# Two layers of local attention and a token-mixing MLP on one core: the last output projection summed in two parts, residual rows loaded in place, probability rows padded in DRAM

## The chip, the cores and the metric

One core of a Trainium2 chip runs the whole program. The metric is device time in microseconds of one launch. Several runs of a kernel are compared by their medians; a profile is one further execution, recorded by the hardware.

## The reference

Four residual blocks on a sequence of 2048 rows of 1024 numbers (bf16): attention A, MLP B, A, B, each after a layer norm.

```python
x = x + _A_ref(_layernorm(x), A_wqkv, A_wo)
x = x + _B_ref(_layernorm(x), B_w1, B_b1, B_w2, B_b2)
x = x + _A_ref(_layernorm(x), A_wqkv, A_wo)
x = x + _B_ref(_layernorm(x), B_w1, B_b1, B_w2, B_b2)
```

`_A_ref` has 32 heads of 32 numbers. A position s looks at the 8 positions s, s-2, ..., s-14: 8 logits, a softmax, a weighted sum of 8 values, then the product with `wo`. `_B_ref` mixes along the sequence: `u = gelu(h^T w1 + b1)` with 3584 hidden numbers for each of the 1024 columns, `y = u w2 + b2`, transposed back.

## The kernel before

Because the attention's step is 2, even and odd positions never meet: the kernel holds them as two classes (`c` = 0 and 1) of 1024 rows, eight row tiles of 128 each. Rows of a layer-normed class are turned into `hT` (features on partitions).

**Attention.** The 1024 features are eight feature tiles (`dt`), in two groups of four; a class and a group make a step n = 0 to 3 of `Attn.stream`. For a step, TensorE (PE) projects q, k and v per feature tile (`project`, L398 to L416; ScalarE, ACT, copies each bank out). `qk` (L431): VectorE (DVE) multiplies q by four windows of k into a tile T, twice per feature tile, and PE sums T over the head's 32 features by a 0/1 matrix `sel` into the logits `sc` (L444). `softmax_front` and `softmax_back` (L449, L458) turn these into probabilities Pb on DVE and ACT. Pb goes to a DRAM scratch `pd` and is read back twice by POOL's queue as `pb` (`spread`, L474), spread over the partitions of each head: 16 rows of 16 KB in `pd`, each read by eight partitions. `pv` (L485) multiplies `pb` by windows of v on DVE and adds up eight products (L500 to L506) into `oT`, the attention output with features on partitions, in two halves (`hf`) of 512 positions. The work of `pv` for step n-1 lies beside `qk` of step n; the PV of the last step stands alone at the end of the stream.

**Output projection.** `out_proj` (L591) computes, for each of eight row tiles, two sums (one for each 512 columns) of eight matmuls over the eight `oT` tiles, into a PSUM bank each; DVE adds the residual row `xr` (L626 or L629), POOL's queue stores the row to `xa`, and the row is normalized into `h2`, by ACT (class 0, `on_act`) or by DVE (class 1). There are six banks in the pool `ps`, shared by all such sums. Class 0's projection lies beside attention of class 1; class 1's follows the last PV.

**MLP.** `gemm1` sums over row tiles of `h2`; the sums over class 0's rows for ten of fourteen blocks are done early (`partials`), as filler. `gemm2_tile` (L670) makes a row tile of the output from 28 hidden tiles in two banks, and adds bias and residual `xs` into `xo` on DVE (L687). In layer 0 class 0's tiles come first and class 1's are filler beside layer 1's attention.

**What sets the order.** `weave` (L715) goes through the attention's units in a plan with guessed costs: units `"pe"` and `"dve"` carry a cost, names they wait for, names they set. Where a unit must wait in the plan, it pulls filler (class 1's rows and values, class 0's output projection, the partial sums) until PE's planned time has come. The plan only ranks the work: a scheduler then orders each engine's instructions, and each engine runs its own in that order. DMAs are issued in order by queue: SP issues all loads and transposes, POOL the stores, `pd` and `pb`. An issue that has to wait for a buffer holds up what is queued behind it.

**Buffers.** Five weight buffers (`wb`: class 1's value weights `wv`, `wo`, `w1`, `w2`), three of `wq`, four row buffers (`x2`: `xr`, `xn`, `xs`, `xo`, `hb`), two for T and the PV products, two of `pb`. Each pool goes round in turn.

Of the kernel before, what the change touches and what calls it, by code (L numbers as in the profile page):

```python
# [26 lines left out]
def kernel(  # L27
# [37 lines left out]
    HF = FT // NW2  # L65
    SLACK = 0.5
    PB_LAG = 12.0
    OUT0_GAP = 7.0
    assert D == H * DH and W == 8 and SC == 1024 and HD * KD == H and SB * CH == 32
    scale = float(DH) ** -0.5  # L70
# [98 lines left out]

    xa = [[dram.tile([SC, D], BF16, name=f"xa{li}{c}") for c in range(DIL)] for li in range(2)]  # L170
    xb = [dram.tile([SC, D], BF16, name=f"xb{c}") for c in range(DIL)]
    pd = [dram.tile([P, W * TB], BF16, name=f"pd{n}") for n in range(2 * DIL * NCQ)]

    xin_v = x_in.rearrange("(i m c) d -> c i m d", m=P, c=DIL)
    out_v = out2d.rearrange("(i m c) d -> c i m d", m=P, c=DIL)
# [173 lines left out]
    class Attn:  # L349
# [81 lines left out]
        def qk(self, n, dq):  # L431
            c, dt = n // NCQ, (n % NCQ) * DQ + dq
            if dq == 0:
                self.sc = pssp.tile([P, 2, 4, TB], FP32, name="sc", tag="sc")
            q, k = self.q_of(c, dt), self.k_of(c, dt)
            for par in range(2):
                yield "dve", 2.2, [("ready", 0, dt), ("ready", 1, dt)], [("free", x, dt % 2) for x in range(2)] if par and not self.apart(c, dt) else [], 0.0, 0.6
                T = tpl.tile([P, 4, SC], BF16, name="T", tag="T")
                nc.vector.tensor_tensor(out=T[:], in0=q.unsqueeze(1).to_broadcast([P, 4, SC]),  # L439
                                        in1=window(k, par, 2, [(2, 4), (1, SC)]), op=ALU.mult)  # L440
                for sb in range(SB):
                    for gr in range(4):
                        b = SB * gr + sb
                        nc.tensor.matmul(self.sc[32 * gr:32 * gr + 32, par], lhsT=sel[:, sb * DQ + dq, :],  # L444
                                         rhs=T[:, :, b * TB:(b + 1) * TB],
                                         start=(dq == 0 and sb == 0), stop=(dq == DQ - 1 and sb == SB - 1))
# [11 lines left out]
        def softmax_back(self, n):  # L458
            yield "dve", 3.0, ["exp"], [("pb", n, 0)], PB_LAG, 0.0
            yield "dve", 0.0, [], [("pb", n, 1)], PB_LAG + 6.0, 0.0  # L460
            nc.vector.tensor_tensor(out=m4[:], in0=L[:, 0:4, :], in1=L[:, 4:8, :], op=ALU.add)
            nc.vector.tensor_tensor(out=m4[:, 0:2, :], in0=m4[:, 0:2, :], in1=m4[:, 2:4, :], op=ALU.add)
            nc.vector.tensor_tensor(out=m4[:, 0, :], in0=m4[:, 0, :], in1=m4[:, 1, :], op=ALU.add)
            nc.vector.reciprocal(out=m4[:, 1, :], in_=m4[:, 0, :])
            nc.vector.tensor_tensor(out=Pb[:], in0=L[:], in1=m4[:, 1:2, :].to_broadcast([P, W, TB]), op=ALU.mult)
            base = self.pd(n)[0, 0]
            dst = bass.AP(base.tensor, base.offset, [(W * TB, 4 * SB), (4 * SB * W * TB, CH), (1, W * TB)])
            nc.gpsimd.dma_start(out=dst, in_=Pb[:].rearrange("p u t -> p (u t)"))
            self.spread(n)

# [3 lines left out]
        def spread(self, n):  # L474


            for hf in range(2):
                pb = pbp.tile([P, 4, W, TB], BF16, name="pb", tag="pb")
                self.pbs[(n, hf)] = pb
                base = self.pd(n)[4 * hf, 0]  # L480
                src = bass.AP(base.tensor, base.offset, [(4 * SB * W * TB, CH), (0, P // CH), (1, 4 * W * TB)])
                nc.gpsimd.dma_start(out=pb[:].rearrange("p b u t -> p (b u t)"), in_=src)

        def pv(self, n, half, hf, dqs=(0, 1)):
# [3 lines left out]
            for dq in (2 * half + x for x in dqs):  # L488
# [20 lines left out]
        def stream(self, lead):  # L509
# [77 lines left out]
            for half in range(2):  # L587
                for hf in range(2):
                    yield from self.pv(last, half, hf)

    def out_proj(at_, c, res, dst, h2, on_act):  # L591

        if not on_act:
            yield "pe", 0.0, ["oT"], [], 0.0
        dst_v = rows(dst)
        wo_t = [[None, None] for _ in range(NDC)]
        for n in range(NDC):
            for hf in range(2):
                wt = wb("wo", [P, KD // 2, 512])
                nc.sync.dma_start(out=wt[:], in_=wo_v[hf, :, :, n * 512:(n + 1) * 512])  # L600
                wo_t[n][hf] = wt
        for hf in range(2):
            h2[c][hf] = hx(f"h2{c}{hf}", [P, NT // 2, D])
        xrs = []

        def fetch():
            if len(xrs) < NT:
                xrs.append(x2("xr"))
                nc.sync.dma_start(out=xrs[-1][:], in_=res[len(xrs) - 1])

        fetch()
        fetch()
        for i in range(NT):
            if not on_act:
                yield "pe", 3.5, ["oT"], [], 3.6
            xr = xrs[i]
            xn = x2("xn")
            s1 = st("s1", [P, NDC]) if on_act else None
            for n in range(NDC):
                ps = bank()  # L620
                xs_ = slice(n * 512, (n + 1) * 512)
                for kt in range(KD):
                    nc.tensor.matmul(ps[:], lhsT=at_.oT[c][kt][:, i * P:(i + 1) * P], rhs=wo_t[n][kt // 4][:, kt % 4, :],  # L623
                                     start=(kt == 0), stop=(kt == KD - 1))
                if on_act:
                    nc.vector.scalar_tensor_tensor(out=xn[:, xs_], in0=ps[:], scalar=1.0, in1=xr[:, xs_], op0=ALU.mult,  # L626
                                                   op1=ALU.add, accum_out=s1[:, n:n + 1])
                else:
                    nc.vector.tensor_tensor(out=xn[:, xs_], in0=ps[:], in1=xr[:, xs_], op=ALU.add)  # L629
            fetch()  # L630
            nc.gpsimd.dma_start(out=dst_v[i], in_=xn[:])  # L631
            h = h2[c][i // 4][:, i % 4, :]
            if on_act:
                nm, rs = stats_act(xn[:], 1.0 + EPS, eps2, h, s1)
                norm_act(h, xn[:], nm, rs)
                yield 3.5, 0.0
            else:
                mean, rs = stats_dve(xn[:], 1.0 + EPS, eps2)
                norm_dve(h, xn[:], mean, rs)

    def w1_tile(c, fb):
        t = wb("w1", [P, NT, FB])
# [25 lines left out]
                    nc.scalar.activation(out=gs, in_=tmp[:], func=ACT.Gelu_apprx_tanh, bias=b1_sb[:, ft:ft + 1])  # L668
                yield 0.216 * nk, 0.0

    def gemm2_tile(c, i, w2t, src, dst, hT, on_act=False, end=False):
        xs = x2("xs")
        nc.sync.dma_start(out=xs[:], in_=src[c][i * P:(i + 1) * P, :])
        xo = x2("xo")
        halves = [slice(n * 512, (n + 1) * 512) for n in range(NDC)]
        groups = [halves[:1], [slice(512, 768)], [slice(768, 1024)]] if end else [halves]
        for cols in groups:
# [7 lines left out]
                    yield 1.5 * len(cols), 0.0  # L685
            for ps, xc in zip(acc, cols):
                nc.vector.scalar_tensor_tensor(out=xo[:, xc], in0=ps[:, 0:xc.stop - xc.start], scalar=b2_sb[:, i, c:c + 1],  # L687
                                               in1=xs[:, xc], op0=ALU.add, op1=ALU.add)
# [25 lines left out]
    def run(*its):  # L714
        for _ in chain(*its):  # L715
            pass

    def weave(lead, fills, lags):
# [6 lines left out]
        def pull(force=False):  # L725
# [13 lines left out]
                        opened[y] = when[f]  # L739
            return False  # L740

        def reach(t):
            nonlocal pe
            while pe < t - SLACK:
                if not pull():
                    pe = min([t] + [x for x in list(opened.values())[:1] if x > pe])
            pe = max(pe, t)

        for kind, *unit in lead:
# [7 lines left out]
                pe, dve = unit  # L757
            elif kind == "pe":
                cost, waits, sets, then = unit
                reach(max([pe] + [when.get(w, 0.0) for w in waits]))  # L760
                pe += cost
                when.update((x, pe + 2.0) for x in sets)
                if then:
                    dve = max(dve, pe) + then
            else:
                cost, waits, sets, lag, then = unit
                dve = max([dve] + [when.get(w, 0.0) for w in waits]) + cost
                if then:
                    reach(dve)
                    pe += then  # L770
# [11 lines left out]
    for li in range(2):  # L782
# [21 lines left out]

        def second_class():
            new_hT(hT, 1)
            for i in range(NT):
                if first:
                    prologue_tile(1, i, hT)
                    yield 0.0, 2.0 * (i % 2 == 0)  # L810
                else:
                    yield from gemm2_tile(1, i, w2_tiles(i), xa[0], xb[1][i * P:(i + 1) * P, :], hT, on_act=i < NT - 2)

        def v_ahead():
            if not first:
# [18 lines left out]
        if first:  # L834
            with at(top):
                ln_exp_table()
            hT = [[None, None] for _ in range(DIL)]
            new_hT(hT, 0)
            for i in range(NT):
                run(gemm2_tile(0, i, w2_tiles(i), xa[0], xb[0][i * P:(i + 1) * P, :], hT))  # L840
        else:
            for i in range(NT):
                w2t = w2_tiles(i)
                for c in range(DIL):
                    run(gemm2_tile(c, i, w2t, xa[1], out_v[c, i], None, end=(i == NT - 1 and c == DIL - 1)))


# [28 lines left out]
```

## Time and profile before

| | |
|---|---|
| median of 17 runs | 1321.79 us (1317.19 to 1325.72) |
| profiled execution | 1317.19 us, its span 1315.4 us |
| mean granted TensorE clock | 0.992 of full |
| PE, DVE, ACT busy | 1279.4, 682.5, 439.3 us |
| moved by DMA | 173 MB |

A page gives busy times, a chain of work, groups of instructions and DMA issues. The timeline gives each stretch of like instructions with its start and length in us, and in brackets how long the engine had stood before it and what released it. The list of waits adds these up: total, times, longest. Engines work beside one another, so an idle engine costs time only where its work sets the end.

### The profile page before, as it was taken

The numbers are of one execution on the slowest core, as the hardware profiler recorded it, in microseconds if no ns is written. First come the engines' busy times: TensorE is split into PE (matmuls) and PEld (weight loads), VectorE is DVE, ScalarE is ACT, GpSimd is POOL, SyncE is SP. The second block draws the span as 40 slices with busy tenths as digits, with TensorE's granted clock in tenths as the row PEclk, the third lists the DMA queues.
The fourth block names the chain that finished last, engine by engine and source line by source line (L and its number), as shares of the span: only waits on it lengthen the run. The fifth ranks groups of instructions, "written<-read, shape, count | busy, mean of one in ns | idle before, by whom it ended". The sixth has DMA issues, their size and how long they took to land. (4 is left out here: it accounts for less than half of the span.)

```text
span 1315.4 us, 15470 instructions
## 1 busy us (share of the span) xinstructions
PE 1279.4 (97%) x6284; PEld 575.7 (44%) x6284; DVE 682.5 (52%) x861; ACT 439.3 (33%) x740; POOL 61.2 (5%) x166
## 2 busy tenths in 40 slices
PE   9998899998999999999999999999899999999999
PEld 5343343443444444444444444444344444444444
DVE  6879789989202332334697844879940033111011
ACT  6844355731313420023534435475132144000000
POOL 3000001000000000000000000010000000000000
PEclk9998899999999999999999999999999999999999
DMA  9752426552523238863659862348262322334332
GB/s 256 168 124 62 112 81 168 176 152 96 145 66 95 76 112 219 218 173 119 165 148 237 213 177 64 88 129 216 73 184 65 85 76 72 118 100 135 118 110 69
DMA packets 243544, 173.00 MB, mean 132 GB/s; under 512 B 32208, under 2 KB 227152, under 8 KB 241424
## 3 DMA queue, kind: packets, MB, share of 16 engines
q1 hardware_dynamic: 233648, 133.45, 37.5%
q0 software_dynamic: 9248, 37.51, 10.2%
q8 instruction: 49, 0.80, 0.3%
q10 hardware_dynamic: 576, 1.05, 0.2%
q14 instruction: 23, 0.19, 0.1%
HBM read 146.81 MB, written 18.87 MB: 126 GB/s over the span
## 5 line engine op out<-in xcount | busy, mean ns | idle before, releaser
L682 PE MATMUL ps<-g,w 128*128 128x512 bf16 (+1 forms) x1820 | 389.7, 376 | 2.8 <-DVE xo L687 2.8
L656 PE MATMUL ps<-h,w 128*128 128x512 bf16 x1792 | 388.1, 379 | 2.7 <-ACT h L230 2.4
L682 PEld LDWEIGHTS <-w 128*128 128x128 bf16 x1820 | 177.5, 98 | 213.1 <-issue 6.1
L656 PEld LDWEIGHTS <-w 128*128 128x128 bf16 x1792 | 175.3, 98 | 214.9 <-issue 3.9
L409 PE MATMUL ps<-hT,wq 128*128 128x512 bf16 (+1 forms) x1112 | 243.8, 376 | 1.0 <-issue 0.5
L667 DVE TENSOR_TENSOR tmp<-ps,g 128x512 f32<-128x512 f32 x80 | 55.3, 692 | 233.1 <-PE ps L656 233.1
L687 DVE SCALAR_TENSOR_TENSOR xo<-ps,b_sb,xs 128x512 bf16<-128x512 f32 (+1 forms) x65 | 45.6, 738 | 247.7 <-PE ps L682 237.0
L439 DVE TENSOR_TENSOR T<-q,k 128x4096 bf16<-128x4096 bf16 x60 | 135.9, 2287 | 67.0 <-ACT q L413 54.0
L409 PEld LDWEIGHTS <-wq 128*128 128x128 bf16 x1112 | 108.8, 100 | 131.4 <-issue 13.8
L504 DVE TENSOR_TENSOR pr<-pr 128x2048 bf16<-128x2048 bf16 (+1 forms) x128 | 119.2, 947 | 0.1
L409 PE MATMUL ps<-hT,wv 128*128 128x512 bf16 x448 | 104.0, 385 | 5.7 <-DMA wv<-in_A_wqkv_dram 5.7
L623 PE MATMUL ps<-wo,oT 128*128 128x512 bf16 x384 | 93.1, 385 | 11.2 <-DVE oT L506 8.3
L500 DVE TENSOR_TENSOR pr<-pb,v 128x2048 bf16<-128x2048 bf16 x64 | 76.0, 1214 | 24.6 <-DMA pb<-pd 14.4
L416 ACT CAST k<-ps 128x1024 bf16<-128x1024 f32 x60 | 60.8, 1016 | 76.3 <-PE ps L409 76.3
L668 ACT ACTIVATE g<-tmp,b_sb 128x512 bf16<-128x512 f32 x80 | 57.7, 722 | 82.4 <-DVE tmp L667 82.4
L500 DVE TENSOR_TENSOR pr<-pb,g 128x2048 bf16<-128x2048 bf16 x64 | 76.4, 1216 | 7.8 <-DMA pb<-pd 7.8
L409 PEld LDWEIGHTS <-wv 128*128 128x128 bf16 x448 | 48.8, 112 | 58.0 <-issue 8.4
L662 ACT CAST g<-ps 128x512 bf16<-128x512 f32 x80 | 45.6, 589 | 67.7 <-PE ps L656 67.7
L623 PEld LDWEIGHTS <-oT 128*128 128x128 bf16 x384 | 37.1, 99 | 61.7 <-issue 10.7
L192 ACT ACTIVATE ln<-mv,eps 128x1 f32<-128x1 f32 x37 | 10.9, 295 | 158.7 <-DVE mv L201 151.2
L413 ACT CAST q<-ps 128x512 bf16<-128x512 f32 x60 | 35.0, 585 | 51.7 <-PE ps L409 51.7
L416 ACT CAST g<-ps 128x1024 bf16<-128x1024 f32 x36 | 36.5, 1017 | 47.2 <-PE ps L409 47.2
(91 smaller groups left out, 598.8 us busy)
## 6 DMA issues: line engine op xcount, KB each, us to landing
w<-in_B_w_dram SPq DMA_DIRECT2D x96, 448.0 KB, 3.8
w<-in_B_w_dram SPq DMA_DIRECT2D x56, 512.0 KB, 4.4
wq<-in_A_wqkv_dram SPq DMA_DIRECT2D x38, 512.0 KB, 4.0
pb<-pd POOLq DMA_DIRECT2D x16, 1024.0 KB, 10.9
wo<-in_A_wo_dram SPq DMA_DIRECT2D x16, 512.0 KB, 4.5
xa<-xn POOLq DMA_DIRECT2D x32, 256.0 KB, 3.6
xs<-xa SPq DMA_DIRECT2D x32, 256.0 KB, 4.1
wv<-in_A_wqkv_dram SPq DMA_DIRECT2D x14, 512.0 KB, 5.6
```

Source lines behind the costliest of these rows:

```text
L409: nc.tensor.matmul(ps[:, lo:hi], lhsT=cols, rhs=self.hT[c][hf][:, kt, lo:hi], start=(kt == 0), stop=(kt == KD - 1))
L416: nc.scalar.copy(out=window(buf, 0, PADK + hf * HT, [(KW + 1, 2), (1, HT)]), in_=ps[:].unsqueeze(1).to_broadcast([P, 2, HT]))
L439: nc.vector.tensor_tensor(out=T[:], in0=q.unsqueeze(1).to_broadcast([P, 4, SC]), in1=window(k, par, 2, [(2, 4), (1, SC)]), op=ALU.mult)
L500: nc.vector.tensor_tensor(out=pr[:, :, u, :], in0=pb[:, :, u, :], in1=window(self.v_of(c, dt), par, 2 + hf * HT, [(TB, 4), (2, 4), (1, TB) ...
L504: nc.vector.tensor_tensor(out=pr[:, :, 0:wd, :], in0=pr[:, :, 0:wd, :], in1=pr[:, :, wd:2 * wd, :], op=ALU.add)
L623: nc.tensor.matmul(ps[:], lhsT=at_.oT[c][kt][:, i * P:(i + 1) * P], rhs=wo_t[n][kt // 4][:, kt % 4, :], start=(kt == 0), stop=(kt == KD - 1))
L656: nc.tensor.matmul(ps[:], lhsT=wt[c][:, i, fl * P:(fl + 1) * P], rhs=h2[c][i // 4][:, i % 4, dc * 512:(dc + 1) * 512], start=(k == 0), sto ...
L662: nc.scalar.copy(out=gs, in_=ps[:])
L667: nc.vector.tensor_tensor(out=tmp[:], in0=ps[:], in1=gs, op=ALU.add)
L668: nc.scalar.activation(out=gs, in_=tmp[:], func=ACT.Gelu_apprx_tanh, bias=b1_sb[:, ft:ft + 1])
L682: nc.tensor.matmul(ps[:, 0:xc.stop - xc.start], lhsT=w2t[n][:, ft % HF, c::DIL], rhs=g[ft // GF][:, ft % GF, xc], start=(ft == 0), stop=(f ...
L687: nc.vector.scalar_tensor_tensor(out=xo[:, xc], in0=ps[:, 0:xc.stop - xc.start], scalar=b2_sb[:, i, c:c + 1], in1=xs[:, xc], op0=ALU.add, ...
```

## The change

- `out_proj` for class 1: the sums of the first three row tiles over feature tiles 0 to 5 (six banks, 36 matmuls) are issued before the last `oT` tiles are there; the last two feature tiles are added after. In the plan this unit is placed by the half-finished last PV (`("oT", 0)`) and by the end of the last PV plus 6 us. Even row tiles of class 1 have their statistics and norm on ACT, odd ones on DVE.
- `Rows`: residual rows are loaded ahead (three in `out_proj`, two in `gemm2_tile`), and the addition writes into the buffer that the row was loaded into; `xn` and `xo` are gone.
- In `qk` of the first step of a layer the plan no longer waits for DVE (its `then` cost is 0), and PE's 0.6 us are a unit of their own.
- `pd` has rows of 17 KB in place of 16 KB (512 numbers of padding behind each); what is written and read is the same.

```diff
+    PDW = 4 * SB * W * TB + 512
-    pd = [dram.tile([P, W * TB], BF16, name=f"pd{n}") for n in range(2 * DIL * NCQ)]
+    pd = [dram.tile([CH, PDW], BF16, name=f"pd{n}") for n in range(2 * DIL * NCQ)]
...
             for par in range(2):
-                yield "dve", 2.2, [...], [...], 0.0, 0.6
+                yield "dve", 2.2, [...], [...], 0.0, 0.6 * bool(n)
+                if n == 0:
+                    yield "pe", 0.6, [], [], 0.0
...
-            dst = bass.AP(base.tensor, base.offset, [(W * TB, 4 * SB), (4 * SB * W * TB, CH), (1, W * TB)])
+            dst = bass.AP(base.tensor, base.offset, [(W * TB, 4 * SB), (PDW, CH), (1, W * TB)])
...
-                base = self.pd(n)[4 * hf, 0]
-                src = bass.AP(base.tensor, base.offset, [(4 * SB * W * TB, CH), (0, P // CH), (1, 4 * W * TB)])
+                base = self.pd(n)[0, 4 * hf * W * TB]
+                src = bass.AP(base.tensor, base.offset, [(PDW, CH), (0, P // CH), (1, 4 * W * TB)])
...
-                yield "dve", 4.7, waits, [("free", 2, dt % 2), "oT"] if hf else [], 0.0, 0.0
+                yield "dve", 4.7, waits, [("free", 2, dt % 2), "oT", ("oT", half)] if hf else [], 0.0, 0.0
...
+    class Rows:
+        def __init__(self, srcs, depth):
+            self.srcs, self.depth = iter(srcs), depth
+            self.tiles = []
+        def take(self):
+            while len(self.tiles) <= self.depth:
+                src = next(self.srcs, None)
+                if src is None:
+                    break
+                self.tiles.append(x2("xr"))
+                nc.sync.dma_start(out=self.tiles[-1][:], in_=src)
+            return self.tiles.pop(0)

     def out_proj(at_, c, res, dst, h2, on_act):
-        if not on_act:
-            yield "pe", 0.0, ["oT"], [], 0.0
+        early = 0 if on_act else 3
+        if early:
+            yield "pe", 1.28 * early * NDC, [("oT", 0), ("less", "oT", -6.0)], [], 0.0
...
+        def multiply(i, n, kts):
+            if (i, n) not in banks:
+                banks[(i, n)] = bank()
+            for kt in kts:
+                nc.tensor.matmul(banks[(i, n)][:], lhsT=at_.oT[c][kt][:, i * P:(i + 1) * P],
+                                 rhs=wo_t[n][kt // 4][:, kt % 4, :], start=(kt == 0), stop=(kt == KD - 1))
+        def kts(i):
+            return range(KD - 2 if i < early else 0, KD)
+        for i in range(early):
+            for n in range(NDC):
+                multiply(i, n, range(KD - 2))
+        xrs = Rows([res[i] for i in range(NT)], 2)
         for i in range(NT):
-            if not on_act:
-                yield "pe", 3.5, ["oT"], [], 3.6
-            xr = xrs[i]
-            xn = x2("xn")
+            if early:
+                yield "pe", 0.43 * len(kts(i)), ["oT"], [], 3.6
+                on_act = i % 2 == 0
+            xn = xrs.take()
...
-                    nc.vector.tensor_tensor(out=xn[:, xs_], in0=ps[:], in1=xr[:, xs_], op=ALU.add)
-            fetch()
+                    nc.vector.tensor_tensor(out=xn[:, cols], in0=ps[:], in1=xn[:, cols], op=ALU.add)
...
-    def gemm2_tile(c, i, w2t, src, dst, hT, on_act=False, end=False):
-        xs = x2("xs")
-        nc.sync.dma_start(out=xs[:], in_=src[c][i * P:(i + 1) * P, :])
-        xo = x2("xo")
+    def gemm2_tile(c, i, w2t, xs, dst, hT, on_act=False, end=False):
+        xo = xs.take()
...
-                                               in1=xs[:, xc], op0=ALU.add, op1=ALU.add)
+                                               in1=xo[:, xc], op0=ALU.add, op1=ALU.add)
...
+        def ready(t, waits):
+            for w in waits:
+                t = max(t, when[w[1]] - w[2] if w[0] == "less" else when.get(w, 0.0))
+            return t
```

Each caller of `gemm2_tile` makes its `Rows` with a depth of 1; `weave` uses `ready` where it took the latest of a unit's waits itself.

More of the change, by code (lines that the diff above doesn't have):

```diff
@@ L436, in qk @@
             for par in range(2):
-                yield "dve", 2.2, [("ready", 0, dt), ("ready", 1, dt)], [("free", x, dt % 2) for x in range(2)] if par and not self.apart(c, dt) else [], 0.0, 0.6
+                yield "dve", 2.2, [("ready", 0, dt), ("ready", 1, dt)], [("free", x, dt % 2) for x in range(2)] if par and not self.apart(c, dt) else [], 0.0, 0.6 * bool(n)
+                if n == 0:
+                    yield "pe", 0.6, [], [], 0.0
                 T = tpl.tile([P, 4, SC], BF16, name="T", tag="T")
@@ L603, in out_proj @@
             h2[c][hf] = hx(f"h2{c}{hf}", [P, NT // 2, D])
[L604 to L609, printed above, removed]
-        fetch()
-        fetch()
+        banks = {}
+        def multiply(i, n, kts):
[4 more added lines that the diff above has]
+                                 rhs=wo_t[n][kt // 4][:, kt % 4, :], start=(kt == 0), stop=(kt == KD - 1))
@@ L618, in out_proj @@
             s1 = st("s1", [P, NDC]) if on_act else None
             for n in range(NDC):
[L620 to L624, printed above, removed]
+                cols = slice(n * 512, (n + 1) * 512)
+                multiply(i, n, kts(i))
@@ L625, in out_proj @@
+                ps = banks.pop((i, n))
                 if on_act:
-                    nc.vector.scalar_tensor_tensor(out=xn[:, xs_], in0=ps[:], scalar=1.0, in1=xr[:, xs_], op0=ALU.mult,
+                    nc.vector.scalar_tensor_tensor(out=xn[:, cols], in0=ps[:], scalar=1.0, in1=xn[:, cols], op0=ALU.mult,
                                                    op1=ALU.add, accum_out=s1[:, n:n + 1])
                 else:
-                    nc.vector.tensor_tensor(out=xn[:, xs_], in0=ps[:], in1=xr[:, xs_], op=ALU.add)
@@ L630, in out_proj @@
-            fetch()
+                    nc.vector.tensor_tensor(out=xn[:, cols], in0=ps[:], in1=xn[:, cols], op=ALU.add)
             nc.gpsimd.dma_start(out=dst_v[i], in_=xn[:])
@@ L635, in out_proj @@
                 norm_act(h, xn[:], nm, rs)
-                yield 3.5, 0.0
             else:
@@ L639, in out_proj @@
                 norm_dve(h, xn[:], mean, rs)
+            if not early:
+                yield 3.5, 0.0
     def w1_tile(c, fb):
@@ L759, in weave @@
                 cost, waits, sets, then = unit
-                reach(max([pe] + [when.get(w, 0.0) for w in waits]))
+                reach(ready(pe, waits))
                 pe += cost
@@ L766, in weave @@
                 cost, waits, sets, lag, then = unit
-                dve = max([dve] + [when.get(w, 0.0) for w in waits]) + cost
+                dve = ready(dve, waits) + cost
                 if then:
@@ L806, in second_class @@
             new_hT(hT, 1)
+            xs = Rows([rows(xa[0][1])[i] for i in range(NT)], 1)
             for i in range(NT):
@@ L811, in second_class @@
                 else:
-                    yield from gemm2_tile(1, i, w2_tiles(i), xa[0], xb[1][i * P:(i + 1) * P, :], hT, on_act=i < NT - 2)
+                    yield from gemm2_tile(1, i, w2_tiles(i), xs, xb[1][i * P:(i + 1) * P, :], hT, on_act=i < NT - 2)
         def v_ahead():
@@ L838 @@
             new_hT(hT, 0)
+            xs = Rows([rows(xa[0][0])[i] for i in range(NT)], 1)
             for i in range(NT):
-                run(gemm2_tile(0, i, w2_tiles(i), xa[0], xb[0][i * P:(i + 1) * P, :], hT))
+                run(gemm2_tile(0, i, w2_tiles(i), xs, xb[0][i * P:(i + 1) * P, :], hT))
         else:
+            xs = Rows([rows(xa[1][c])[i] for i in range(NT) for c in range(DIL)], 1)
             for i in range(NT):
@@ L844 @@
                 for c in range(DIL):
-                    run(gemm2_tile(c, i, w2t, xa[1], out_v[c, i], None, end=(i == NT - 1 and c == DIL - 1)))
+                    run(gemm2_tile(c, i, w2t, xs, out_v[c, i], None, end=(i == NT - 1 and c == DIL - 1)))
 _INS = ['A_x', 'A_wqkv', 'A_wo', 'B_x', 'B_w1', 'B_b1', 'B_w2', 'B_b2']
```

## The prediction

> **What bounds the kernel now.** I read the page first, then PE's waits, then PE's timeline with DVE's and SP's beside it. The page's first part says which engine to keep a ledger of:
>
> ```profile
> span 1315.4 us, 15470 instructions
> PE 1279.4 (97%) x6284; PEld 575.7 (44%) x6284; DVE 682.5 (52%) x861; ACT 439.3 (33%) x740; POOL 61.2 (5%) x166
> ```
>
> TensorE is idle for 1315.4 - 1279.4 = 36.0 us in all. The change neither adds nor removes a matmul, so it can only move those 36 us and the microseconds lost to slow matmuls behind a wait. The list of PE's waits says where they are:
>
> ```profile
> PE ps L623 <- DVE oT L506: 8.3, 3, 3.7
> PE sc L444 <- DVE T L439: 6.5, 4, 5.0
> PE ps L409 <- DMA wv<-in_A_wqkv_dram: 5.7, 1, 5.7
> PE ps L623 <- DMA wo<-in_A_wo_dram: 3.0, 2, 2.4
> PE ps L682 <- DVE xo L687: 2.8, 1, 2.8
> PE ps L656 <- ACT h L230: 2.4, 3, 1.8
> ```
>
> PE's timeline places them (start, length, then in brackets the wait before):
>
> ```profile
> 102.02 1.04 PE L444 MATMUL sc<-T,sel 128*32 128x512 bf16 x8 [4.97 <-DVE T L439]
> 103.00 2.75 PE L409 MATMUL ps<-hT,wv 128*128 128x512 bf16 x6
> 145.49 1.90 PE L409 MATMUL ps<-hT,wv 128*128 128x512 bf16 x4 [5.66 <-DMA wv<-in_A_wqkv_dram]
> 204.41 1.02 PE L623 MATMUL ps<-wo,oT 128*128 128x512 bf16 x4 [2.36 <-DMA wo<-in_A_wo_dram]
> 303.13 0.39 PE L623 MATMUL ps<-wo,oT 128*128 128x512 bf16 x1 [2.88 <-DVE oT L506]
> 712.28 15.05 PE L682 MATMUL ps<-g,w 128*128 128x512 bf16 x69 [2.80 <-DVE xo L687]
> 934.37 0.39 PE L623 MATMUL ps<-wo,oT 128*128 128x512 bf16 x1 [3.70 <-DVE oT L506]
> 944.26 1.02 PE L623 MATMUL ps<-wo,v 128*128 128x512 bf16 x4 [0.73 <-DVE xn L629]
> 961.52 157.29 PE L656 MATMUL ps<-h,w 128*128 128x512 bf16 x728
> ```
>
> DVE's and SP's rows beside them:
>
> ```profile
> 99.68 2.29 DVE L439 TENSOR_TENSOR T<-q,k 128x4096 bf16<-128x4096 bf16 x1
> 102.33 6.70 DVE L439 TENSOR_TENSOR T<-q,k 128x4096 bf16<-128x4096 bf16 x3
> 312.28 0.68 DVE L629 TENSOR_TENSOR xn<-ps,xr 128x512 bf16<-128x512 f32 x1
> 198.62 0.55 SPq L600 DMA_DIRECT2D wo<-in_A_wo_dram  x1
> ```
>
> The first three: T is computed one after the other on DVE, and the additions that free output banks come after DVE's last PV. The fourth: SP issues the last wo tile at 198.62, when its buffer falls free; PE waits for it until 204.41.
>
> PE's last row gives the undisturbed rate: 157.13 us to the next row for 728, 0.216 us each. PE's second row shows the price behind a wait: six matmuls in 2.75 us where seven take 1.69 elsewhere. Added up from the rows behind each wait against their undisturbed twins, 2.1 us are lost so after 4.97, 2.3 after 5.66, 1.6 after 2.36, and 1.5 at 303.
>
> **The change, part by part.** Durations are from the profiled execution: 1317.19 us, its span plus 1.8. It is the lowest of 17 runs, 4.6 under their median of 1321.79; I sum against it and add 4.6.
>
> *The planner, layer 0.* Charging no fill to the first group's products shifts PE's whole built order. Ahead of the selection at 102.02 there are now 168 projection matmuls since 63.33, not 144. These 24 take 5.2 us, so PE gets there at 102.2, when the first T (99.68 plus 2.29) is done. But the second T's selection now follows at once, and DVE ends that T at about 104.5: a new wait of 1.75. The wait for wv was a load issued at 131.85, beside pb's reads, that took 13.6 us. In the new order its buffer falls free at about 124.4, before those reads, and the tile is needed at 129.7; the rows of wv land in 3.5 to 5.6 us, so I take 0 (bounds 0 and 1). The output projection of class 0 then begins near 185.8 instead of 199.3, and its oT (192.8 less DVE's lead of 8.5, from T groups ending at 171.1 instead of 179.6) is there at 184.3.
>
> *The new wait, for wo.* Behind five shared weight buffers, only the fourth wo tile waited for the last V projection of class 1 (issued 198.62; wait 2.36). In the new order that projection stands right ahead of the output projection, and the second and third wo tile wait for its buffers: SP issues them at 184.9 and 185.8, behind them two wq loads that stood in its queue, then the fourth wo. A lone wo lands in 3.8 us at best; while w streams (500 to 580 us) the DMA moves 233 GB/s at a share of 0.88, 265 if full, so 512 KB more take 2.0 us. The fourth lands at 184.9 + 3.8 + 4 x 2.0 = 196.7. PE can do 15 matmuls meanwhile (189.1): 7.6 us of waits, plus 1.6 slow. Bounds: 2.4 (the row of before) and 14 (the longest landing of a wo, 14.1); 7.6 is nearest to five loads in a row.
>
> *DVE behind it.* DVE's queue holds the addition of the second output tile half ahead of the next T, so DVE waits too (193.8 to 198.0), and PE's selections after it. Counting DVE's queue on with its own rows (T 2.2, pr 1.13 and 0.6, addition 0.69), it starts the next PV group at 211.3 against 217.46, loses 2.1 more to waits on output sums, and keeps a lead of 4.1, of which slow matmuls take 0.9: the last PV of layer 0 ends at 310.0 against 313.2.
>
> *The early sums, layer 0.* 128 matmuls from 298.80 to 332.61 need 27.6 us and take 33.8. Now 24 more partial matmuls of the MLP come first (5.2 us), then 36 early ones, which need only oT tiles ready by 285, then 12 that need the last oT. PE has these done at about 307, but then all six banks are full, and the first is freed only by an addition after DVE's last PV: 310.7. So the wait for oT becomes one of 3.7 for a bank, with 1.3 us slow. The other 80 matmuls (17.3) end at 329.3. Gain: 332.6 - 329.3 + 5.2 = 8.5, in which every wait and gain of layer 0 so far is already contained, because DVE sets this point.
>
> *Layer 1, middle.* The 2.80 at 712 is PE without a bank: DVE stands at a product waiting for pb, with two evictions behind it. In the new order four evictions stand ahead of that product. I take 2.3 gained (0 to 2.8), since two more switches between selection and fill cost 0.1 each, and the first selections lose about 0.3.
>
> *Layer 1, end.* 128 matmuls take 32.5 us instead of 27.6. With 24 partial and 36 early ones first, PE comes to the twelve at 929.0 + 5.2 + 7.8 = 942.0; oT is there at 934.3. They end at 944.6; the last PV ends at 942.8, the first bank is free at 943.5. No wait: 4.6 gained.
>
> *Rows in place.* Loads, bytes and DVE instructions are the same, so no term. What is new: a row load waits for the store of an earlier tile, and SP issues nothing meanwhile. In the MLP of layer 0 the store lands 5 us after the tile and the load stood behind a transpose at 4.8 already; at layer 1's worst place (behind pb on POOL) a w tile is issued near 704 and needed at 715.8, and lands in 3.8: slack 8. (There POOL's store of the second row tile moves behind the second group's pd write and pb reads, some 6 us of waiting for that write; the row load that needs its buffer is three tiles on.) Cost 0; if the slack goes, it is the third rival. Half of class 1's tiles take their statistics on ACT: 3.9 us each there, 2.0 less on DVE, beside 72 and 128 partial matmuls (15 and 27 us).
>
> *Padded rows.* At 78 to 84 us, pb's reads nearly alone move 225 to 242 GB/s with DMA full; 265 would save 1 us of a pair's 8.9. DVE waits on pb before layer 0's last PV group, so 0 to 1 us; I take 0, as the DMA is as busy with w.
> [...]
>
> [...]
>
> Sum: 8.5 + 2.3 + 4.6 = 15.4; 1317.2 - 15.4 = 1301.8, as a median 1306.4.
>
> **The rivals.**
> 1. DVE keeps no lead (0.2). If the fourth wo lands at 201 or later, DVE's last PV ends at 313.2 as before and layer 0 gives 5.2. With 1 us gained in layer 1's middle: 5.2 + 1 + 4.6 = 10.8, 1311. For: every landing above 10 us fell beside pb, and a pd write is near. Against: pb starts only after that write.
> 2. The loads are quicker (0.15). With the fourth wo at 192 and pb 1 us faster, DVE ends near 305 and PE has no wait for a bank: 13.5 + 2.3 + 4.6, 1301.4.
> 3. Slower (0.07). SP stuck behind stores: at the three probability reads that overlap row loads in layer 1, the store would have to land over 8 us later than counted. At 7 us of PE each, 21 lost against 15.4 gained: 1327. It decides from 6 us each. Against: stores land in 3.3 to 3.6.
> 4. Nothing moves (0.05): early sums with banks held only turn the wait for oT into one for a bank in both layers, and the wo wait eats what the planner gives: 1320. Against: layer 1's first bank is free before it is needed.
>
> **How the numbers follow.** The forecast has 0.53. Measurement can tell 0.2%, 2.6 us. Faster: 0.53 + 0.2 + 0.15 = 0.88; same 0.05; slower 0.07. The range, 1298 to 1317, takes in the first two rivals and the bounds of wo; rival 3, most of 4 and some of the bounds' tails lie outside.
>
> **What would show it.** PE: a short wait for T near 102 and none for wv; a new wait for wo of 5 to 10 us at about 187 to 197; in layer 0 a wait for the addition's bank near 307, none for oT; in layer 1 none at either. Layer 0's output projection ends near 329 and layer 1's close to where it did in PE's order less 7 to 15 us. I am wrong if DVE ends layer 0's PV later than 313, if weights of layer 1's MLP arrive late behind SP, or if wv waits again.

## The result and the profile after

The changed kernel takes 1305.89 us (median of 10 runs, 1303.53 to 1309.71) against 1322.01 for the kernel before in all its runs (59): a ratio of 0.9881, 95% interval 0.9867 to 0.9895. That is 16.1 us less; 15.4 were forecast, and the time itself was forecast as 1306.4. The sum came out right, but two of its terms did not: between the two profiles layer 0 gained 5.5 us more than predicted and the middle of layer 1 6 us less. The profiled execution took 1303.53 us, the lowest of its ten, and 13.66 less than the profiled one of before, the second lowest of its 59.

The first part of the page of after:

```profile
span 1301.7 us, 15529 instructions
PE 1274.6 (98%) x6284; PEld 575.0 (44%) x6284; DVE 669.6 (51%) x845; ACT 463.7 (36%) x788; POOL 60.9 (5%) x166
```

PE stands idle for 27.1 us in place of 36.0, and its busy time fell by 4.8. The list of PE's waits in after (in total, times, longest) shows what is left:

```profile
PE ps L629 <- DVE xr L650: 5.2, 2, 4.9
PE sc L447 <- DVE T L442: 3.4, 4, 2.0
...
PE ps L629 <- DMA wo<-in_A_wo_dram: 2.1, 2, 1.5
PE ps L704 <- ACT v L417: 1.9, 3, 0.9
PE ps L410 <- DVE xr L709: 1.8, 2, 1.1
...
PE ps L680 <- DMA w<-in_B_w_dram: 0.9, 1, 0.9
PE ps L704 <- DMA w<-in_B_w_dram: 0.8, 1, 0.8
```

The waits for `oT` (8.3) and `wv` (5.7) are gone, the one for `wo` has shrunk, and one of 4.9 for an output bank is new. PE's timeline of after has them in place:

```profile
104.85 0.61 PE L447 MATMUL sc<-T,sel 128*32 128x512 bf16 x8 [2.05 <-DVE T L442]
...
185.97 3.40 PE L629 MATMUL ps<-wo,oT 128*128 128x512 bf16 x15
190.84 7.28 PE L629 MATMUL ps<-wo,oT 128*128 128x512 bf16 x33 [1.47 <-DMA wo<-in_A_wo_dram]
...
304.46 1.86 PE L629 MATMUL ps<-wo,v 128*128 128x512 bf16 x4 [4.88 <-DVE xr L650]
...
323.82 1.89 PE L680 MATMUL ps<-h,w 128*128 128x512 bf16 x8
326.65 18.52 PE L680 MATMUL ps<-h,w 128*128 128x512 bf16 x85 [0.94 <-DMA w<-in_B_w_dram]
...
698.50 9.01 PE L704 MATMUL ps<-g,w 128*128 128x512 bf16 x41 [0.33 <-ACT v L417]
...
715.32 3.61 PE L410 MATMUL ps<-hT,wq 128*128 128x512 bf16 x16 [1.15 <-DVE xr L709]
719.80 0.38 PE L704 MATMUL ps<-g,w 128*128 128x512 bf16 x1 [0.87 <-ACT v L417]
...
935.82 1.02 PE L629 MATMUL ps<-wo,v 128*128 128x512 bf16 x4 [0.28 <-DVE xr L650]
...
953.08 152.11 PE L680 MATMUL ps<-h,w 128*128 128x512 bf16 x704
```

Layer 0's last projection ends at 323.8 (332.6 before), with 24 more partial products done, 5.2 us: 14.0 gained. DVE's timeline shows what PE stood for at 304:

```profile
303.37 0.42 DVE L509 TENSOR_TENSOR oT<-pr 128x512 bf16<-128x512 bf16 x1
303.71 0.68 DVE L650 SCALAR_TENSOR_TENSOR xr<-ps,xr 128x512 bf16<-128x512 f32 x1
```

The last PV ends at 303.8 and the first addition frees a bank at 304.4. In layer 1's middle one wait of 2.80 has become a row of small ones (3.7 in all from 682 to 721). At layer 1's end only 0.28 is left.

From these rows the ledger of the two profiles is: layer 0 to the end of the last projection +14.0; the wait for `w` at 326 and its slow matmuls -1.1; from layer 1's first projection to class 0's output projection -3.7 (284.5 us before, 288.1 after); the last projection +4.5 (32.5 and 28.1). Together 13.7.

### The profile page after: what moved, and what is told of

It reads as the page before. It is cut to its first block, busy times and chain, and to the rows that moved or that the text cites. A ratio compares the mean times of both kernels' runs of the same rounds, so it can differ in the third digit from the quotient of the medians.

```text
span 1301.7 us, 15529 instructions
## 1 busy us (share of the span) xinstructions
PE 1274.6 (98%) x6284; PEld 575.0 (44%) x6284; DVE 669.6 (51%) x845; ACT 463.7 (36%) x788; POOL 60.9 (5%) x166
## 3 DMA queue, kind: packets, MB, share of 16 engines
q10 hardware_dynamic: 576, 1.05, 0.2%
## 5 line engine op out<-in xcount | busy, mean ns | idle before, releaser
L709 DVE SCALAR_TENSOR_TENSOR xr<-ps,b_sb,xr 128x512 bf16<-128x512 f32 (+1 forms) x65 | 45.6, 738 | 251.4 <-PE ps L704 219.4
L503 DVE TENSOR_TENSOR pr<-pb,v 128x2048 bf16<-128x2048 bf16 x64 | 76.0, 1215 | 23.2 <-ACT v L417 11.7
L688 ACT ACTIVATE g<-ps,b_sb 128x512 bf16<-128x512 f32 x32 | 22.0, 687 | 83.2 <-PE ps L680 83.2
```

The source lines that it names most:

```text
L503: nc.vector.tensor_tensor(out=pr[:, :, u, :], in0=pb[:, :, u, :], in1=window(self.v_of(c, dt), par, 2 + hf * HT, [(TB, 4), (2, 4), (1, TB) ...
```

## Experiments

The theory after the result: (1) the planner's change and the early sums both shorten PE's stand ahead of layer 0's last projection; (2) something in the change, not its order alone, costs layer 1's middle some 4 us. Rivals are named with each run. Every kernel's profile was cut at the same points (us; starts of rows of PE's timeline):

| kernel | median | ratio to before, 95% | last projection of layer 0 | layer 1's middle | last projection of layer 1 |
|---|---|---|---|---|---|
| before | 1322.01 | | 298.8 to 332.6 | 284.5 | 32.5 |
| before, second profile | 1324.27 | 1.0016 [0.9997, 1.0036] | 299.8 to 333.6 | 287.3 | 34.5 |
| after | 1305.89 | 0.9881 [0.9867, 0.9895] | 289.1 to 323.8 | 288.1 | 28.1 |
| after_again | 1306.29 | 0.9868 [0.9849, 0.9886] | 293.5 to 328.4 | 289.3 | 27.6 |
| one_row | 1306.16 | 0.9867 [0.9847, 0.9887] | 290.7 to 325.7 | 289.0 | 27.6 |
| rows_fresh | 1303.78 | 0.9844 [0.9825, 0.9862] | 290.5 to 325.0 | 289.0 | 27.6 |
| plan_old | 1310.16 | 0.9901 [0.9886, 0.9916] | 304.6 to 332.3 | 288.9 | 27.6 |
| plan_only | 1312.43 | 0.9932 [0.9915, 0.9949] | 288.7 to 326.0 | 288.5 | 33.2 |
| sum_late | 1312.63 | 0.9933 [0.9915, 0.9951] | 286.0 to 323.3 | 289.2 | 32.5 |
| pb_reuse | 1299.19 | 0.9827 [0.9807, 0.9847] | 291.5 to 326.3 | 282.9 | 27.6 |
| two_pools | 1299.97 | 0.9831 [0.9808, 0.9854] | 291.3 to 326.5 | 283.8 | 27.6 |
| no_pad | 1306.40 | 0.9878 [0.9857, 0.9898] | 289.7 to 324.3 | 290.1 | 28.5 |
| norm_dve | 1305.42 | 0.9868 [0.9843, 0.9892] | 293.6 to 328.9 | 289.1 | 27.6 |
| pools_fill | 1293.59 | 0.9785 [0.9764, 0.9806] | 294.6 to 322.3 | 283.6 | 27.6 |

Where the early sums are in, 24 more partial products (5.2 us) stand ahead of the last projection, in pools_fill 48. Layer 0's points differ by 4.4 and 4.6 us between the two executions of the changed kernel, so they are read together. The groups of runs stood beside different runs of the kernel before, whose median went from 1321.5 to 1324.7, so between groups the ratios count as well as the medians. In all traces but those of before and after some 120 matmul records are missing; the starts of rows stand.

**after_again.** 

> The changed kernel once more, unaltered, as the yardstick for the other three of this group. It should stand at 0.988 of the kernel before (1305.9 against 1322.0, interval 0.9867 to 0.9895), some 16 us less. In its trace the third class-1 row tile of layer 1's MLP is normalized on ACT after a wait of about 7 us for the store of the second tile, VectorE then waits some 8 us for a v eviction behind it, and layer 1's middle ends about 3.7 us later than the kernel before would from the same start. If that was an accident of one execution, the wait is gone here.

The same again: ACT waited 7.4 us for the store and DVE 6.3 behind it; the middle took 289.3.

**one_row.**

```diff
-            xs = Rows([rows(xa[0][1])[i] for i in range(NT)], 1)
+            xs = Rows([rows(xa[0][1])[i] for i in range(NT)], 0)
```

> Only the row loads of layer 1's class-1 MLP tiles are taken one at a time instead of two ahead (depth 0 in place of 1); the addition still goes into the loaded buffer. Theory A (the row buffers: the normalized tile hb goes into the buffer of the row stored just before, so ACT stands until that store has landed, with the evictions of v behind it): ACT's wait for the store goes and 3 to 4 us with it, about 1302 to 1303. Theory B (PE's new order, with more evictions ahead of the PV product, costs layer 1's middle, and the buffers have no part): no change, 1306. Theory C (a row loaded late now arrives late): slower, 1308 or more.

No change in time, as Theory B had it, yet this decides nothing: ACT's wait went, but in the built order two additions slid behind the product that waits for `pb`, and PE stood for their banks instead. PE's timeline of one_row:

```profile
696.16 3.24 PE L410 MATMUL ps<-hT,wq 128*128 128x512 bf16 x7 [3.53 <-DVE xr L709]
```

**rows_fresh.**

```diff
-            xn = xrs.take()
+            xr = xrs.take()
+            xn = x2("xn")
...
-        xo = xs.take()
+        xr = xs.take()
+        xo = x2("xo")
```

with `xr` as the additions' input, and depths 1 and 0. 

> The addition writes into a fresh tile again (xn, xo), and rows are loaded one ahead in the output projection and none ahead in the MLP, all through; the rest as in the changed kernel. Theory A: 3 to 4 us gained in layer 1's middle, and another 1 to 2 since no row load stands behind a store in SP's queue ahead of weights (waits of 0.9 and 0.8 us for w in the changed kernel): 1301 to 1303. Theory B: 1306. Theory C (loading ahead in place is worth something): 1308 or more.

2.5 us less than after_again, the two intervals overlapping. The middle is unchanged (289.0), by the same slide as in one_row. PE's list of waits has none for `w`, where after has 0.9 and 0.8. So loading ahead in place bought nothing here.

**plan_old.**

```diff
-... [], 0.0, 0.6 * bool(n)
-                if n == 0:
-                    yield "pe", 0.6, [], [], 0.0
+... [], 0.0, 0.6
```

> The planner's unit of the first group is put back as before (PE's fill charged again); early sums, rows and padding stay. Theory A (the planner gives most of layer 0's gain: the waits of 4.97 for T and 5.66 for wv with their slow matmuls, 2.4 at wo): those waits come back, the last PV of layer 0 ends near 313, and with the early sums layer 0 keeps only their 24 earlier products, 5.2 us: some 8 us slower than the changed kernel, 1314. Theory B (DVE sets the end of layer 0 anyway and the early sums give its gain): 1307 to 1309. Layer 1's end keeps its 4.5 us in both.

3.9 us slower than after_again by the medians, between the two theories. The waits for T and `wv` are back (5.0 and 6.4) and the last projection begins near 304.6, but with the sums split it runs through to 332.3.

**before_again.** 

> The kernel before once more, for a second profile of it. From layer 1's first projection to class 0's output projection the shown profile of before took 284.5 us; the changed kernel and three of its variants took 288.1 to 289.3 there, whatever their rows and planner. Theory A (the shown execution was lucky: its second pb of layer 1 landed 9.4 us after its issue, and PE's wait of 2.80 stayed too short to cost slow matmuls): here pb takes 10 to 12, PE stands 4 to 5.5 us, and the stretch takes 287 to 289. Theory B (something in the changed kernel costs 4 us there): 284 to 285 again.

Theory A, for the most part: the first read of that pair landed 11.0 us after its issue, and PE stood 4.09 there. The middle took 287.3, near the 288 to 290 of the changed kernels. The last projection took 34.5 against 32.5: its wait for `oT` was 4.04 in place of 3.70, and matmuls were slow behind it (the granted clock was 0.50 from 937.04 to 943.87). PE's timeline of before_again at the two places:

```profile
714.60 2.62 PE L682 MATMUL ps<-g,w 128*128 128x512 bf16 x7 [4.09 <-DVE xo L687]
...
938.49 0.61 PE L623 MATMUL ps<-wo,oT 128*128 128x512 bf16 x1 [4.04 <-DVE oT L506]
```

So the first profile of before was some 5 us better than this one at these two places (2.8 and 2.0).

**pb_reuse.**

```diff
             for hf in range(2):
+                if self.li == 1 and n == 1:
+                    self.pbs[(n, hf)] = self.pbs[(0, hf)]
+                    continue
                 pb = pbp.tile([P, 4, W, TB], BF16, name="pb", tag="pb")
```

> The changed kernel with the second pair of pb reads of layer 1 left out: the second PV group multiplies the first group's probabilities again, so the output is not the reference's. The order of all other instructions is the same. Theory A (layer 1's middle is bound by that read, with the additions that free PE's banks queued behind the product that waits for it on DVE): no wait for pb, no wait of PE for a bank there, and 3 to 5 us less, 1301 to 1303. Theory B (ACT's wait for the row store binds): that wait goes too, since the store no longer lands beside the reads, but PE's waits for v evictions stay; 1305 to 1306.

Without the second pair of reads the middle takes 282.9, and the time falls by 7 us (5 by the ratios): the reads and what lands beside them do hold it. But this also takes away what made the row store land late, so it cannot tell the wait for `pb` from the wait for the store: here that store landed 2.9 us after its issue, in after 12.4.

**two_pools.**

```diff
-    x2p = pool("x2p", 4)
+    x2p = pool("x2p", 2)
...
+    turn = [0]
-    def x2(name, shape=None, dt=BF16):
-        return x2p.tile(shape or [P, D], dt, name=name, tag="x2")
+    def x2(name, shape=None, dt=BF16, side=None):
+        if side is None:
+            turn[0] += 1
+        return x2p.tile(shape or [P, D], dt, name=name, tag=f"x2{turn[0] % 2 if side is None else side}")
...
-                self.tiles.append(x2("xr"))
+                self.tiles.append(x2("xr", side=self.side))
...
-        hb = x2("hb")
+        hb = x2("hb", side=1)
```

with side 0 for the rows of the two MLP stages that make `hb`. 

> The changed kernel with its four row buffers split into two pairs: the MLP's loaded rows go round in one pair, the normalized tiles hb in the other (other tiles alternate). No hb takes the buffer of a row that is being stored; PE's order is the same, and the additions that free banks stay ahead of the product that waits for pb. Loading one row at a time took ACT's wait away too and gained nothing, but there two additions stood behind that product. Theory A (ACT's wait for the store, with the v evictions behind it, binds layer 1's middle once the additions are out of the way of pb): no wait of ACT for a store, PE's waits for v evictions and banks between 680 and 722 shrink from some 4 us to under 1.5, and 2 to 4 us less: 1302 to 1304, 0.985 to 0.987 of before. Theory B (pb alone binds; DVE's later work follows it in any case): 1306, 0.988. Theory C (row loads now wait for the store two tiles back and arrive late): over 1307.

Theory A, and more than it asked: 6 us less than the changed kernel, and than no_pad and norm_dve of the same group. ACT's timeline shows the cause. First after, then two_pools:

```profile
687.66 1.24 ACT L231 ACTIVATE hb<-xr,bi,rs 128x1024 bf16<-128x1024 bf16 x1
696.22 0.63 ACT L213 ACTIVATE hb<-xr 128x512 bf16<-128x512 bf16 x1 [7.32 <-DMA xb<-xr]
...
697.46 0.99 ACT L417 CAST v<-ps 128x1024 bf16<-128x1024 f32 x1
```

```profile
688.08 0.62 ACT L217 ACTIVATE hb<-xr 128x512 bf16<-128x512 bf16 x1
...
694.01 0.99 ACT L421 CAST v<-ps 128x1024 bf16<-128x1024 f32 x1
```

In after the third class-1 tile's `hb` lies in the buffer of the second tile's row, whose store was issued at 683.5, beside `pb`'s two megabytes, and landed only at 696; a copy of `v` out of its bank stands behind it on ACT. POOL's row of after with the issue, 12.4 us ahead of the landing:

```profile
683.54 0.58 POOL L715 DMA_DIRECT2D xb<-xr  x1 [1.53 <-DVE xr L709]
```

In two_pools the same store took even longer, 13.5 us, and nothing waited for it. What the wait did to DVE, again after first:

```profile
689.11 1.23 DVE L503 TENSOR_TENSOR pr<-pb,v 128x2048 bf16<-128x2048 bf16 x1 [4.20 <-DMA pb<-pd]
698.48 2.36 DVE L503 TENSOR_TENSOR pr<-pb,v 128x2048 bf16<-128x2048 bf16 x2 [8.15 <-ACT v L417]
```

```profile
686.56 1.39 DVE L713 SCALAR_TENSOR_TENSOR xr<-ps,b_sb,xr 128x512 bf16<-128x512 f32 x2
694.60 3.50 DVE L507 TENSOR_TENSOR pr<-pb,v 128x2048 bf16<-128x2048 bf16 x3 [6.66 <-DMA pb<-pd]
```

DVE waits for `pb` longer in two_pools (6.66 against 4.20) and nobody minds: the additions that free PE's banks begin at 686.56, ahead of it, and the 8.15 behind ACT are gone. PE's timeline of two_pools from 683 to 730 has one wait, 0.91 at 685.09. So the cost of the middle was neither PE's order alone nor `pb` alone: with this order it was the row buffer, and where two additions stand behind the product (one_row, rows_fresh) PE's 3.5 and 3.9 us there come from `pb`, as their rows read.

**no_pad.** `PDW = 4 * SB * W * TB`. 

> The changed kernel without the padding: rows of the probability scratch 16 KB apart as before. Theory A (padding does nothing: undisturbed pairs of reads landed 6.9 and 12.3 us after issue with 16 KB, 7.1 and 12.6 with 17 KB): 1305 to 1307, 0.987 to 0.988 of before. Theory B (a power-of-two pitch slows these reads): the pairs take 1 us or more longer and the time is 1308 to 1310.

Theory A: 1306.40. Undisturbed pairs land 6.9 and 12.5 us after issue without padding, 7.1 and 12.6 with it in after.

**norm_dve.** The line `on_act = i % 2 == 0` left out. 

> The changed kernel with the norms of all class-1 row tiles on VectorE, as before. Theory A (no term, as predicted: DVE's additions keep ahead of PE after the last PV): 1305 to 1307. Theory B (with three row tiles of additions at once, DVE's norms between them hold banks back): additions come later in both layers, PE waits for banks among the last 80 matmuls, 1307 to 1310.

Theory A: 1305.42; PE's waits in the two last projections are those of the changed kernel (5.0 for a bank in layer 0, none in layer 1).

**sum_late.**

```diff
-        early = 0 if on_act else 3
-        if early:
-            yield "pe", 1.28 * early * NDC, [("oT", 0), ("less", "oT", -6.0)], [], 0.0
+        early, last = 0, not on_act
+        if last:
+            yield "pe", 0.0, ["oT"], [], 0.0
```

> No early sums: class 1's output projection sums all eight feature tiles in one go again and stands in the plan as before; planner, rows, norms and padding as in the changed kernel. Theory A (the early sums are worth what the prediction gave them): in layer 0 PE comes to the projection near 285, stands some 9 us for oT (until about 294), fills six banks and ends it 3 to 4 us later than now, in layer 1 the 4.5 us come back: 1313 to 1315. Theory B (DVE's last PV sets layer 0's end, only layer 1's end counts): 1310 to 1311. Theory C (banks held early give nothing): 1306.

6.3 us slower than after_again by the medians, a little under Theory A, and 8.6 by the ratios, within it. PE stands 6.7 and 3.3 us for `oT`, the longer at 296:

```profile
296.13 1.04 PE L629 MATMUL ps<-wo,oT 128*128 128x512 bf16 x2 [6.73 <-DVE oT L509]
```

The split sums cut this stand to 4.8, so in layer 0 they bring about 2 us of it, which is less than layer 0's points vary by, and in layer 1 the whole 4.9.

**plan_only.** The diff of plan_old the other way round, in the kernel before. 

> The kernel before with the planner's unit changed and nothing else. Undoing it in the changed kernel cost 4 us (1310.2 against 1306.3), and the early sums have to be worth the rest. Theory A (both shorten the same stretch, PE's stand ahead of layer 0's last output projection, so either alone gives most of it): the waits for T and wv shrink, the last PV ends near 304, the projection ends near 322 instead of 332.6, and the time is 1311 to 1314. Theory B (the parts add up): 4 us gained, 1319 to 1321.

Theory A in the time, though the projection ended at 326.0 and not near 322: 1312.43, some 9 us gained by this alone (9.6 by the medians, 9.0 by the ratio), though its removal from the changed kernel cost only 4. The gains overlap: with the last PV at its old place the sums fill PE's stand, and with the PV earlier there is less to fill.

**pools_fill.** two_pools with `("less", "oT", -11.0)` in place of -6.0. 

> The kernel with two pairs of row buffers, and the early sums placed 5 us of plan time later: 24 more partial products of the MLP stand ahead of them in either layer. In layer 0 PE has stood 4.7 to 5.1 us in every run with early sums, at six full banks, until DVE's last PV is done and its first addition frees one. Theory A (that wait is only PE being early, and the work that fills it is taken from behind): the wait shrinks to under 1.5 us, the slow matmuls after it go, layer 1 keeps its place: 5 to 6 us less than 1300.0, 1294 to 1295.5. Theory B (DVE's additions, not the last PV, pace what follows): the wait only moves to later banks, 1298 to 1300. Theory C (in layer 1 the products are wanted later): over 1300.

Theory A: 1293.59, 2.15% under the kernel before (interval 1.94 to 2.36) and the fastest version of all. The wait for a bank in layer 0 is gone (of the other runs with early sums only plan_old had none, since its last projection began at 304.6); PE's timeline of pools_fill runs through where after stood 4.88:

```profile
301.95 3.19 PE L633 MATMUL ps<-wo,oT 128*128 128x512 bf16 x14
305.06 1.02 PE L633 MATMUL ps<-wo,v 128*128 128x512 bf16 x3
```

DVE had just freed that bank; the 24 products that fill the time come from behind the projection, where they cost as much. The mean granted clock of this run is 1.000.

## Why the prediction was right, and where it was not

*What bounds the kernel.* Right: nothing but PE's waits (8.9 us less) and the slow matmuls behind them (4.8 less busy time) moved.

*T, `wv`, class 0's projection.* Right to a fraction: the second T's wait was 2.05 (1.75 predicted), `wv` none, the projection began at 185.97 (185.8).

*The new wait for `wo`.* Wrong, 1.47 us in place of 7.6. The step that failed is "the second and third `wo` tile wait for its buffers", the last V projection's. SP's rows of after show when they were issued:

```profile
165.53 1.40 SPq L619 DMA_DIRECT2D wo<-in_A_wo_dram  x2
...
185.30 0.55 SPq L619 DMA_DIRECT2D wo<-in_A_wo_dram  x1
```

The 40 V products that end at 166.3 gave these two their buffers; only the fourth tile waited for the last V projection, as before the change. That fourth tile landed 5.5 us after its issue and let PE go on at 190.8 where 196.7 was counted, so the row of five loads never formed.

*DVE behind it, and layer 0's gain.* The mechanism held, the size did not. The last PV ended at 303.8, not 310.0, since DVE was not held from 193.8 to 198. The mechanism at the end was as told (six full banks, then a wait for the first addition): 4.88 against 3.7, because PE too was earlier, at the banks at 299.6 instead of 307. The projection ended at 323.8 (329.3): 14.0 gained, not 8.5. This is the second rival's condition (the fourth `wo` by 192, the last PV near 305; its layer 0 gain was 13.5), which had a chance of 0.15, though not its point that PE would have no wait.

How much of this is the one execution? In after_again the fourth `wo` let PE go on at 193.6, with slow matmuls behind it (32 in 8.97 us, where after's 33 take 7.28), DVE stood for 2.1 us behind them, its last PV ended at 308.1, and the projection at 328.4: 9.4 gained against the same profile of before, near the 8.5 predicted. So 14.0 is the upper end: the five profiles of the changed kernel and of one_row, no_pad and norm_dve end this projection between 323.8 and 328.9.

*Layer 1's middle.* Wrong in sign: 2.3 gained was predicted, 3.7 lost was measured between the two profiles, about 1 to 2 against before's second. The wait of 2.80 did go, as told, with four additions ahead of the product; where rows are loaded later (one_row, rows_fresh, plan_only) two of them are behind it again, and PE stands 3 to 4 us there. What failed is the term of the next point: the wait for a store took that place. With that wait removed (two_pools) the middle took 283.8, 0.7 less than in the first profile of before and 3.5 less than in the second.

*Rows in place, cost 0.* Wrong. The prediction followed the new waits on SP alone and never asked who else is given a row's buffer. `hb` is, and ACT waited in the middle of its `v` copies; two_pools, where no `hb` meets a store, is 6 us faster. The size of the wait stood in the profile before: the prediction has stores landing in 3.3 to 3.6 us, but before's store issued at 703.3, beside `pb`'s reads, took 11.7, when no computing engine waited for it. On SP the third rival's mechanism did appear at its smallest: `w` late by 0.9 and 0.8 us, where it decides from 6; no kernel with fresh tiles for the sums (the two profiles of before, plan_only, rows_fresh) has a wait of PE for `w`.

*Layer 1's end.* Right: 4.5 of 4.6. Without early sums this projection took 32.5 to 34.5 us in four profiles, with them 27.6 to 28.5, so that the sums are worth 4 to 7.

*Padding and ACT half.* Right: nothing that the runs can tell for either (0.1 us more and 0.9 less than after_again without them).

So 5.5 us too little in layer 0 and 6.0 too much in layer 1's middle cancelled, and between medians the lucky profile of before helped as well. The second profiles of both kernels, whose spans lie 14.3 us apart, show the same signs in smaller sizes: layer 0 +10.4, the waits for `w` -0.9, the middle -2.0, layer 1's end +6.8. A right total is no proof of its terms.

## What to carry to other kernels

When a tile is reused in place, list every tile that shares its pool: in after the next owner of the buffer waited 7.32 us on ACT until the store had landed, and DVE stood 8.15 us for a copy that was queued on ACT behind it. Work that can run early should be ranked by when its banks come free, not only by when its inputs are there; if PE stands at full banks (4.88 us in after, none in pools_fill), put other work ahead of it. Price the landing of a store from a row with the same traffic beside it, not from the median: beside `pb`'s reads it was 11.7 us in before and 12.4 in after, in the median 3.3 to 3.6. The profile of a single execution can be a lucky one (the first of before was some 5 us better at two places than the second), so a second one, of either kernel, is worth its run.

## What the runs showed of the hardware

The slow matmuls behind before's waits at 102, 145, 204 and 303 lie where the granted clock was 0.50. Short of the span's end, before has four such stretches, 99.63 to 106.45, 144.00 to 150.83, 205.44 to 208.85 and 304.43 to 307.84, and after has one, 301.91 to 308.73: each 3.41 us long or twice that. The four starts in before lie 44.4, 61.4 and 99.0 us apart, 13, 18 and 29 times 3.41. How busy PE was in the 3.41 us ahead sets these apart from the others in the two traces. Three stretches by windows laid on that raster (window, length, then busy us of PE, PEld, DVE, ACT and POOL with instructions, then the granted clock, DMA share and GB/s), in before at 202 and at 932, and in before_again at 934:

```profile
202.03:205.44 3.41, 1.05 (x9) 0.37 (x11) 2.98 (x5) 0.00 (x0) 1.03 (x2) 1.00 1.09 328
205.44:208.86 3.42, 3.42 (x15) 0.94 (x16) 3.25 (x4) 2.50 (x7) 0.59 (x1) 0.50 1.04 208
```

```profile
929.10:932.51 3.41, 1.57 (x8) 0.49 (x5) 3.41 (x4) 0.59 (x1) 0.00 (x0) 1.00 0.62 211
932.51:935.92 3.41, 1.55 (x8) 0.72 (x9) 3.41 (x5) 0.00 (x0) 0.00 (x0) 1.00 0.00 0
935.92:939.34 3.42, 3.42 (x17) 1.44 (x16) 3.42 (x5) 0.00 (x0) 0.00 (x0) 1.00 0.00 0
```

```profile
933.63:937.04 3.41, 0.83 (x4) 0.20 (x2) 3.41 (x5) 0.00 (x0) 0.00 (x0) 1.00 0.41 151
937.04:940.45 3.41, 1.96 (x5) 0.73 (x6) 3.41 (x6) 0.00 (x0) 0.00 (x0) 0.50 0.00 0
```

The wait of 3.70 fell across two pieces of 3.41 us, each left 45 to 46% busy, and the next ran at full clock: four matmuls in 1.03 us. The one of 4.04 left a piece 24% busy, and the next ran at half clock, three matmuls in 1.49. In before and after the five pieces ahead of half clock had 0.83, 0.00, 1.05, 0.39 and 1.09 us of PE's work, 0 to 32%; of the others at full clock, short of the span's end, none was under 44% busy. So a wait of 2.36 at 202 was dear (1.05 of 3.41 us busy, and 17 matmuls in 5.08 us behind it) and one of 3.70 was not. What a piece between 32 and 44% would do, these two traces do not show.
